# Agent attention and a leaky MLP on one core: the rest of the weight product, the linear part and the last weight tile move from the head into block 0

## The chip, the core and the metric

The program runs on one core of a Trainium2 chip. A core has five engines that run side by side and wait for each other by semaphores: TensorE (PE, matrix products; PEld is its loading of weights), VectorE (DVE), ScalarE (ACT), GpSimd (POOL) and SyncE (SP), which here only issues transfers. Each engine takes its instructions in the order in which they were written. The metric is the device time of one execution in microseconds (us). The kernel before took 963.24 us, the median of 3 runs (962.23 to 963.6).

## The reference

Cut to what is computed (2 batches of 12,480 tokens, 128 channels, 49 agents, 2,048 hidden units):

```python
def sm(a, b):                       # softmax of scaled scores
    s = scale * (a @ b.transpose(0, 2, 1))
    e = np.exp(s - s.max(-1, keepdims=True))
    return e / (e.sum(-1, keepdims=True) + 1e-09)
agent_v = sm(agents, k) @ v         # 49 x 128 per batch
x = sm(q, agents) @ agent_v         # 24,960 tokens x 128
h = x @ w_in                        # 128 -> 2,048
return np.maximum(0.01 * h, h) @ w_out
```

The weights arrive as 64-bit floats, everything else as 32-bit floats.

## The kernel before, in words

**What is multiplied.** For each batch the kernel forms M = agent_v @ w_in once, so that a token's hidden values are p @ M, where p are its 49 softmax weights towards the agents. The leaky step is split: 0.99 max(h, 0) goes through w_out (tiles wo_hi, wo_lo), and the linear rest 0.01 h @ w_out is one 128-column product with L = agent_v @ ww, ww = 0.01 w_in @ w_out. Every operand is kept as a high and a low part (m_hi and m_lo, l_hi and l_lo, hi and lo), so each product is three matmuls.

**Blocks.** The tokens go in 52 blocks of 480. A block has 8 steps; step p makes the hidden values of column pair p (256 of the 2,048): mm1 (6 matmul instructions on 64 rows, L748) into a two-bank PSUM tile h, of which there are two; relu on ACT (hi, L761) and on DVE (lo, L762); and, two steps later, mm2 (12 instructions, L778) into the block's output tile. Beside it, in fixed steps written with `at(step, function)`, run the softmax chains of the blocks to come (q_hi to p_dup, on ACT, POOL, PE and DVE) and the attention of the second batch. After each step's relu the `at` work of that step is written down, then mm2.

**The head** is all that comes before the first mm1. It loads k, v, q and the raw weights of batch 0, takes scores of agents against k (k_score; the running maximum k_run; k_copy), the maximum over all of them (k_max0 to k_max3), subtracts it (k_sub), exponentiates (k_exp) and sums up with v (k_av32, on PE), normalises (f_copy, f_den, f_tr, f_avT, f_rec), and makes M in four tiles of 512 columns: m_mm on PE, m_hi_of on ACT, m_lo_of on DVE. Beside that it converts the weights from 64-bit words in eight tiles w0 to w7 (even: w_in, odd: w_out): conv_bits (em and e, L246 and L247) on DVE, conv_mant and conv_exp on ACT (L314; L255 and L256), conv_low (L260), conv_sign (L267) and conv_mul (L274) on DVE, then wo_hi (ACT) and wo_lo (DVE). ww is summed up from transposed tiles of w_in (ww_tr L291, ww_copy L298, ww_mm L304).

**What sets the order.** In the head a planner (class Plan) does: each step has an engine, a cost in ns and the steps it follows; the step that can begin first is written next. Where PE would wait, it writes idle products on zeros (heat, L907). From block 0 on the order is written by hand. Tiles wait by buffers: raw weights, k and v of the head share one ring of 9 buffers (`ld`), so a load waits until the ninth load before it has been used up. The auxiliary PSUM tile (turn_82 or turn_83, the one that the block's output doesn't hold) serves every small product in turn.

Of the kernel before, what the change touches and what calls it, by code (L numbers as in the profile page):

```python
# [18 lines left out]
class Plan:  # L19


    def __init__(self, hop, start):
        self.hop, self.free, self.steps, self.done = hop, dict(start), {}, {}
        self.first = set()

    def add(self, name, eng, cost, fn, args, after):
        self.steps[name] = eng, cost, fn, args, after

    def emit(self, idle):
# [34 lines left out]
def tile_agent_attention_then_leaky_mlp(  # L64
# [31 lines left out]
    P = 128  # L96
# [84 lines left out]
    vr = [const.tile([TP, G, VW], F32R, name=f"vr{i}") for i in range(NVR)]  # L181
# [30 lines left out]
    def load_w(n):  # L212
        t = ld.tile([P, MC, 2], I32, tag="ld", name="w64")
# [82 lines left out]
    def ww_copy(n):  # L296
        t = rp.tile([P, MC], F32, tag="hi", name="wT")
# [160 lines left out]

    def av_zero(b, first):
# [56 lines left out]
    def m_parts(b, n):  # L516
# [5 lines left out]
        c = slice(n * MC, (n + 1) * MC)  # L522
        return m_hi[b][:, c], m_lo[b][:, c]

    def m_mm(b, n, pool=None, ps=None):
        if ps is not None:
            pass
        elif pool is None:
            ps = aux()
        else:  # L530
            if n % 2 == 0:
                mp_pair.append(pair("mp"))
            ps = mp_pair[-1][:, n % 2, :]
        ps, w = (ps, w_in_sb[:, n * MC:(n + 1) * MC]) if n < NM else (ps[:, :C], ww)
# [32 lines left out]
    def k_m(b, n):  # L567
        m_mm(b, n)
# [199 lines left out]
    def mm2(i, p):  # L768
# [15 lines left out]
        if p == NP // 2:  # L784
# [102 lines left out]
    with tc.manual_schedule():  # L887
# [8 lines left out]
        for t in vr:  # L896
            nc.gpsimd.memset(t[:, :, C:C + 1].bitcast(F32), 1.0)
            nc.gpsimd.memset(t[:, :, C + 1:C + 2].bitcast(F32), 0.0)
# [3 lines left out]
        avw.extend(halves(0))  # L902

        def heat(n, start=False):

            for i in range(n if ("wmm", NM - 1) not in plan.done else 0):
# [4 lines left out]
        plan = Plan(HOP, {"pe": 6000, "dve": 6500, "act": 2500, "pool": 5000, "dma": 3000})  # L911
# [4 lines left out]
        for o, a, n in SLOTS:  # L916
# [153 lines left out]
```

## Time and profile before

| | |
|---|---|
| median of 3 runs | 963.24 us (962.23 to 963.6) |
| the profiled execution | 963.1 us, its span 961.2 us |
| PE busy | 945.6 us, 98% of the span |
| DVE busy | 739.9 us, 77% |
| ACT busy | 612.3 us, 64% |
| POOL busy | 385.7 us, 40% |
| mean granted clock of PE | 0.998 of full speed |
| bytes moved by DMA | 70.00 MB, of them 20.87 MB before 70 us |

The span is what the profiler recorded of the program; the device time lies 1.9 us above it. The idle time of PE lies almost all in the first 78 us: PE is taken as busy where a matmul was under way, idle products included.

### The profile page before, as it was taken

How to read it: one execution, taken by the hardware profiler on the slowest of the kernel's cores; microseconds unless marked ns; L12 is line 12 of the kernel's file. 1: busy time of each engine (PE TensorE's matmuls, PEld its weight loads, DVE VectorE, ACT ScalarE, POOL GpSimd, SP SyncE). 2: the span in 40 equal slices, each digit the busy share in tenths (PEclk: the TensorE clock that was granted, in tenths of full speed). 3: DMA queues.
4: the chain of work that ended last, by engine and by line, in shares of the span. 5: the costliest groups of instructions: out<-in, count | busy, mean ns of one | idle time of the engine just before them, and what ended most of it. 6: DMA issues, size and time to landing. Idle time of an engine off the chain costs nothing.

```text
span 961.2 us, 22926 instructions
## 1 busy us (share of the span) xinstructions
PE 945.6 (98%) x9438; PEld 889.4 (93%) x9438; DVE 739.9 (77%) x1071; ACT 612.3 (64%) x907; POOL 385.7 (40%) x561
## 2 busy tenths in 40 slices
PE   8889999999999999999999999999999999999998
PEld 7768888889999999999888999999999999998997
DVE  7967767778888888888777777777777777777774
ACT  5756566656666666666676666666666666666654
POOL 3113233335556566564352434333343433343420
PEclk9999999999999999999999999999999999999999
DMA  9930422222312312321111111211111121112110
GB/s 349 380 140 12 130 79 83 66 60 64 94 53 63 94 53 73 85 63 53 32 42 52 43 53 32 62 32 53 42 43 52 43 53 42 52 42 54 32 42 22
DMA packets 28835, 70.00 MB, mean 73 GB/s; under 512 B 4387, under 2 KB 17955, under 8 KB 28731
## 3 DMA queue, kind: packets, MB, share of 16 engines
q1 hardware_dynamic: 28587, 68.42, 23.1%
q8 instruction: 74, 1.21, 0.6%
q14 instruction: 30, 0.25, 0.1%
q10 hardware_dynamic: 144, 0.12, 0.0%
HBM read 43.46 MB, written 12.78 MB: 59 GB/s over the span
## 4 chain that ended last, share of the span: by engine, by line
PE 95%; DVE 3%; DMA 1%; ACT 1%; SPq 0%; issue 0%; POOL 0%; ACTq 0%
PE turn L778 57%; PE h L748 28%; PE turn L622 2%; PE turn L789 2%; PE turn L355 1%; PE turn L447 1%; PE sc L355 1%; DMA kt<-in_k_dram 1%; DVE s_sb L321 1%; PE turn L471 1%; DVE lo L762 0%; PE mp L537 0%; PE turn L304 0%; DVE run L366 0%; PE turn L907 0%
## 5 line engine op out<-in xcount | busy, mean ns | idle before, releaser
L762 DVE SCALAR_TENSOR_TENSOR lo<-h,hi 128x960 fp32r<-128x960 f32 x416 | 478.8, 1151 | 188.4 <-ACT hi L761 188.4
L761 ACT ACTIVATE hi<-h 128x960 fp32r<-128x960 f32 x416 | 405.5, 975 | 292.6 <-PE h L748 266.6
L778 PE MATMUL turn<-hi,wo_hi 64*128 64x480 f32 x1664 | 410.5, 379 | 0.0
L778 PE MATMUL turn<-hi,wo_lo 64*128 64x480 f32 x1664 | 407.5, 376 | 0.0
L748 PE MATMUL h<-pT,m_hi 64*128 64x480 f32 x1664 | 325.7, 377 | 1.4 <-DVE lo L762 1.4
L778 PE MATMUL turn<-lo,wo_hi 64*128 64x480 f32 x1664 | 324.9, 375 | 0.0
L778 PEld LDWEIGHTS turn<-hi,wo_lo 64*128 64x128 f32 x1664 | 257.2, 184 | 7.6
L778 PEld LDWEIGHTS turn<-hi,wo_hi 64*128 64x128 f32 x1664 | 253.2, 184 | 8.0 <-issue 0.7
L778 PEld LDWEIGHTS turn<-lo,wo_hi 64*128 64x128 f32 x1664 | 228.9, 184 | 8.2
L748 PEld LDWEIGHTS h<-pT,m_hi 64*128 64x128 f32 x1664 | 227.0, 184 | 10.2 <-DVE lo L762 2.2
L748 PE MATMUL h<-pT,m_lo 64*128 64x480 f32 x832 | 232.0, 375 | 0.0
L748 PEld LDWEIGHTS h<-pT,m_lo 64*128 64x128 f32 x832 | 134.2, 184 | 4.6
L321 POOL TENSOR_TENSOR pT<-pt,pT 64x480 fp32r<-64x480 f32 (+1 forms) x52 | 63.7, 1226 | 77.1 <-ACT pT L724 77.1
L667 POOL COPY mx<-mx 32x15 f32<-32x15 f32 (+1 forms) x52 | 10.1, 195 | 188.5 <-DVE mx L662 184.2
L321 POOL TENSOR_TENSOR d<-st,mm 64x375 f32<-64x375 f32 (+1 forms) x52 | 43.8, 841 | 95.6 <-DVE mm L673 95.6
L321 POOL TENSOR_TENSOR qlo<-qt,qhi 128x480 fp32r<-128x480 f32 x52 | 64.0, 1231 | 32.8 <-ACT qhi L585 31.6
L812 POOL TENSOR_TENSOR oT<-oT 128x480 f32<-128x480 f32 x51 | 62.5, 1225 | 13.0 <-issue 10.0
L710 POOL TENSOR_TENSOR pd<-d,rs 64x375 f32<-64x375 f32 (+1 forms) x52 | 42.5, 818 | 31.9 <-DVE rs L705 31.9
L667 POOL COPY sm<-sm 32x15 f32<-32x15 f32 (+1 forms) x52 | 9.8, 189 | 106.3 <-DVE sm L690 106.3
L801 ACT COPY oT<-turn 128x480 f32<-128x480 f32 x102 | 51.9, 561 | 0.4 <-PE turn L778 0.4
L622 PE MATMUL turn<-qhi,a_hl 64*128 64x240 f32 x200 | 43.7, 271 | 1.0 <-ACT turn L607 1.0
L622 PE MATMUL turn<-qlo,a_hl 64*128 64x240 f32 x200 | 43.8, 271 | 0.0
(139 smaller groups left out, 905.2 us busy)
## 6 DMA issues: line engine op xcount, KB each, us to landing
qt<-in_q_dram SPq DMA_DIRECT2D x53, 240.0 KB, 2.9
kt<-in_k_dram SPq DMA_DIRECT2D x26, 480.0 KB, 7.5
out_dram<-oT SPq DMA_DIRECT2D x51, 240.0 KB, 2.0
pT<-pT SPq DMA_DIRECT2D x100, 120.0 KB, 2.3
vt<-in_v_dram SPq DMA_DIRECT2D x13, 520.0 KB, 8.4
vt<-in_v_dram SPq DMA_DIRECT2D x13, 487.5 KB, 4.7
w<-in_w_in_dram SPq DMA_DIRECT2D x4, 512.0 KB, 6.8
w<-in_w_out_dram SPq DMA_DIRECT2D x4, 512.0 KB, 8.0
```

The lines of the kernel that those rows point to most:

```text
L321: eng.tensor_tensor(out=o, in0=x, in1=y, op=ALU.subtract)
L355: nc.tensor.matmul(ps[r, j * NA:(j + 1) * NA], lhsT=k_t[b, c][:, j, r], rhs=a_sb[:, b, :], start=True, stop=True,)
L622: nc.tensor.matmul(s_t[i][:, m, :h], lhsT=a_hl[i // BPB][r], rhs=x[r, m * h:(m + 1) * h], start=(s == 0 and n == 0), stop=(n == 1), skip_g ...
L667: nc.gpsimd.tensor_copy(r[:n, :, 1], r[n:2 * n, :, 0])
L710: nc.gpsimd.tensor_tensor(out=pd[:n, :, :A0], in0=d[:n], in1=w[:n].to_broadcast([n, NT, A0]), op=ALU.mult,)
L748: nc.tensor.matmul(ps[:, g, :NB], lhsT=w[b][r, cols(2 * p + g)], rhs=t[r, x], start=(n == 0), stop=(n == 2),)
L761: nc.scalar.activation(hi, ps, AF.Relu)
L762: nc.vector.scalar_tensor_tensor(out=lo, in0=ps, scalar=0.0, in1=hi.bitcast(F32), op0=ALU.max, op1=ALU.subtract,)
L778: nc.tensor.matmul(o[g][:, :NB], lhsT=w[r], rhs=x[r], start=start, stop=stop)
L789: nc.tensor.matmul(o[g][:, :NB], lhsT=w[b][r], rhs=t[r, x], start=False, stop=False)
L801: nc.scalar.copy(t[:, g], o[g][:, :NB])
L812: nc.gpsimd.tensor_tensor(out=t[:, 0], in0=t[:, 0], in1=t[:, 1], op=ALU.add)
```

## The change

In the head, M stops after its first two tiles of 512 columns, and the first of these is made in two halves of 256 (m_half). The third tile is written right after the planned head (k_m(0, 2, 1)), the fourth in step 2 of block 0. The conversion of w7, the last tile of w_out, stands in steps 0 to 4 of block 0, and so do the last quarter of ww (ww_mm in step 3; ww_part and ww_end add the two sums) and L (step 5); the linear product of block 0 moves from its step 4 to its step 6. The softmax chain of block 1, which had been in block 0, is in the planned head as a whole. Raw weights get four tiles of their own (those that later hold vr), so the ring of 9 serves k and v alone; w7 takes the tile of w3. The load order and the planner's costs are new: a load is now an issue on SP, a trip and a transfer. In block 0 the two auxiliary tiles change places.

```diff
         done = self.done
         while len(done) < len(self.steps):
...
                     continue
                 ready = max((done[a] + self.hop for a in after), default=0)
-                key = max(ready, self.free[eng]), name not in self.first, -rest(name)
+                begin = max(ready, self.free.get(eng, 0))
+                key = begin + self.wait.get(name, 0), -rest(name), begin
                 if best is None or key < best[0]:
                     best = key, name
-            (begin, *_), name = best
-            eng, cost, fn, args, _ = self.steps[name]
-            if eng == idle[0] and begin > self.free[eng] + idle[2]:
+            (_, _, begin), name = best
+            eng, cost, fn, args, _, lag = self.steps[name]
+            if eng == idle[0] and begin > self.free.get(eng, 0) + idle[2]:
                 idle[1](round((begin - self.free[eng]) / idle[2]))
             fn(*args)
-            self.free[eng] = done[name] = begin + cost
+            self.free[eng] = begin + cost
+            done[name] = begin + cost + lag
 
...
 
-    ORDER = "qkwwkkkkkkkwkkkkkwvvvqwvvvvwqvwvvvvvw"
+    ORDER = "qkwwkkkkkkkwkkkkkvqvvvwvvwvwvvwvvvvwq"
     HOP = 90
...
     def aux():
...
     def halves(i):
 
         owner[0] = i
-        return [turns[i % 2][:, g, :] for g in range(2)]
+        return [turns[(i + 1) % 2][:, g, :] for g in range(2)]
 
     def pair(name):
...
     def load_w(n):
-        t = ld.tile([P, MC, 2], I32, tag="ld", name="w64")
+        t = const.tile([P, G * VW // 2, 2], I32, tag=f"vr{n % NVR}", name="w64")
+        t = t[:, :MC, :]
         m = n // 2
         if n % 2 == 0:
...
     def ww_copy(n):
-        t = rp.tile([P, MC], F32, tag="hi", name="wT")
+        if n < NM - 1:
+            t = rp.tile([P, MC], F32, tag="hi", name="wT")
+        else:
+            t = ld.tile([P, MC], F32, tag="ld", name="wT")
...
 
@@ -302,12 +309,19 @@
         for j in range(4):
             f = 4 * n + j
             nc.tensor.matmul(
-                avw[1][:, :C], lhsT=wT[n][:, j * P:(j + 1) * P], rhs=w_out_sb[:, f, :],
-                start=False, stop=(f == NF - 1),
+                avw[1][:, WW], lhsT=wT[n][:, j * P:(j + 1) * P], rhs=w_out_sb[:, f, :],
+                start=(n == NM - 1 and j == 0), stop=(f == NF - 1),
             )
 
+    def ww_part():
+        z = m_lo[1][:, :C]
+        nc.tensor.matmul(avw[1][:, WW], lhsT=z, rhs=z, start=False, stop=True)
+        nc.scalar.mul(ww, avw[1][:, WW], SLOPE)
+
     def ww_end():
-        nc.scalar.mul(ww, avw[1][:, :C], SLOPE)
+        nc.vector.scalar_tensor_tensor(
+            out=ww, in0=avw[1][:, WW], scalar=SLOPE, in1=ww, op0=ALU.mult, op1=ALU.add
+        )
...
 
+    def v_ones(r):
+        t = vr[r] = const.tile([TP, G, VW], F32R, tag=f"vr{r}", name="vr")
+        nc.gpsimd.memset(t[:, :, C:C + 1].bitcast(F32), 1.0)
+        nc.gpsimd.memset(t[:, :, C + 1:C + 2].bitcast(F32), 0.0)
...
             m_hi[b] = const.tile([P, DFF], F32R, tag="wm", name=f"m_hi{b}")
...
+        c = slice(int(n * MC), int(n * MC) + (MC if n == int(n) and b + n else MC // 2))
         return m_hi[b][:, c], m_lo[b][:, c]
 
-    def m_mm(b, n, pool=None, ps=None):
+    def m_half(b, h):
+
+        if h == 0:
+            mp_pair.append(pair("mp"))
+        c = slice(h * MC // 2, (h + 1) * MC // 2)
+        ps = mp_t[b, h / 2] = mp_pair[-1][:, 0, c]
...
+
...
         if ps is not None:
             pass
         elif pool is None:
-            ps = aux()
+            ps = aux2()[:, g, :]
         else:
-            if n % 2 == 0:
...
+        ps, w = (ps, w_in_sb[:, n * MC:(n + 1) * MC]) if n < NM else (ps[:, WW], ww)
         mp_t[b, n] = ps
...
             add(wo_lo[:, f, :], hi[:, g])
-        if p == NP // 2:
...
 
-    early = (0, 0, 0, 0, 0, 1, 1, 2, 2, 3, 4, 4, 5, 5, 6, 6, 6, 6)
+    w7 = 2 * NM - 1
+    at(0, conv_bits, w7)
+    at(0, conv_exp, w7)
+    at(1, conv_mant, w7, nc.scalar)
+    at(1, conv_low, w7)
+    at(1, conv_sign, w7)
+    at(2, k_m, 0, NM - 1, 0)
+    at(2, conv_mul, w7, nc.vector)
+    at(3, ww_mm, NM - 1)
+    at(3, ww_end)
+    at(3, wo_hi_of, w7, nc.scalar)
+    at(4, wo_lo_of, w7)
+    at(5, k_m, 0, NM, 1)
+    for x in range(NVR):
+        at(2 * NP + 2 * x, v_ones, x)
     for i in range(1, NBLK):
         at(NP * i + LAG, o_add, i - 1)
-    for r, (_, fn) in zip(early, chain[2:]):
-        at(r, fn, 1)
     for n in range(2, NBLK):
         for r, fn in chain:
             at(max(NP * n + r, 0), fn, n)
-    for i in range(2, NBLK):
+    for i in range(3, NBLK):
         at(max(NP * i - 20, 0), load_q, i)
-    for n in range(1, NM):
...
-            for i in range(n if ("wmm", NM - 1) not in plan.done else 0):
+            for i in range(n):
...
+            after = list(sent)
+            if what == "w":
+                after += [(y, c - NVR) for y in held["w"] if c >= NVR]
+            elif what != "q":
                 if len(ring) >= LD:
                     x, n = ring[-LD]
-                    after = [(y, n) for y in held[x]]
+                    after += [(y, n) for y in held[x]]
                 ring.append((what, c))
-            after += prev
-            prev = [(what, c)]
-            add((what, c), "dma", cost, fn, (c,), after)
+            sent = [("send", what, c)]
+            add(sent[0], "sp", 450, fn, (c,), after, lag=-HOP)
+            add(("trip", what, c), (what, c), 1500, lambda: None, (), sent)
+            if (what, c) == ("w", 0):
+                cost += 1700
+            add((what, c), "dma", cost, lambda: None, (), [("trip", what, c)] + come, lag=-HOP)
+            come = [(what, c)]
...
+        for n in range(w7):
             r = [("mul", n - RP)] if n >= RP else []
-            add(("bits", n), "dve", 940, conv_bits, (n,), [("w", n)] + r)
...
-            add(("mul", n), "dve", 600, conv_mul, (n, dve), [("low", n), ("sign", n)])
+            add(("sign", n), "dve", 620, conv_sign, (n,), [("exp", n)])
+            add(("mul", n), "dve", 620, conv_mul, (n, dve), [("low", n), ("sign", n)])
...
+                add(("wohi", n), "act", 530, wo_hi_of, (n, act), [("mul", n)])
+                add(("wolo", n), "dve", 600, wo_lo_of, (n,), [("wohi", n)])
...
+        for i in range(2):
+            last = ("q", i)
+            for n, (_, fn) in enumerate(chain):
+                eng, cost = costs[fn]
+                after = [last] + [(("chain", 0, 3 if n else 4))] * (i > 0 and n < 2)
+                add(("chain", i, n), eng, cost, fn, (i,), after)
+                last = ("chain", i, n)
...
+        for m in range(NM):
+            add(("tr", m), "pe", 1150, ww_tr, (m,), [("mul", 2 * m)])
+            add(("wcopy", m), "act", 500, ww_copy, (m,), [("tr", m)])
+            if m < NM - 1:
+                add(("wmm", m), "pe", 1000, ww_mm, (m,), [("wcopy", m), ("mul", 2 * m + 1), "avopen"] + [("wmm", m - 1)] * (m > 0))
...
-            add(fn, eng, cost, fn, (0,), [last] + [("s", NCH - 1, 1), ("wcopy", 1)] * (fn is k_max1))
+            add(fn, eng, cost, fn, (0,), [last] + [("s", NCH - 1, 1)] * (fn is k_max1))
...
-        costs = {
-            q_hi: ("act", 493), q_lo: ("pool", 1158), q_mm: ("pe", 403), q_x: ("act", 451),
...
-        last = ("q", 0)
-        for n, (_, fn) in enumerate(chain):
-            eng, cost = costs[fn]
-            add(("chain", n), eng, cost, fn, (0,), [last])
-            last = ("chain", n)
-        for n, fn in enumerate((q_hi, q_lo)):
-            eng, cost = costs[fn]
-            add(("chain1", n), eng, cost, fn, (1,), [("q", 1), ("chain", 4)] + [("chain1", 0)] * n)
...
-        for n in range(NM):
-            after = [f_avT, f_rec] + [("mm", n - 1)] * (n > 0)
-            add(("mm", n), "pe", 860, m_mm, (0, n, ps_h), after)
-            add(("mhi", n), "act", 520, m_hi_of, (0, n), [("mm", n)])
-            add(("mlo", n), "dve", 600, m_lo_of, (0, n), [("mhi", n)])
-            plan.first |= {("mhi", n), ("mlo", n), ("mm", n)}
-        plan.first |= {f_copy, f_rec, f_avT, f_den, f_tr, k_max0, k_max1d, k_max3}
-        plan.first |= {("run", c) for c in range(NCH)}
-        add("L", "pe", 250, k_m, (0, NM), ["ww", ("mlo", 0)])
+        last = f_avT
+        for n, fn, args in ((0, m_half, (0, 0)), (0.5, m_half, (0, 1)), (1, m_mm, (0, 1, ps_h))):
+            x = 1 if n < 1 else 2
+            add(("mm", n), "pe", 435 * x, fn, args, [last])
+            add(("mhi", n), "act", 120 + 240 * x, m_hi_of, (0, n), [("mm", n), f_rec])
+            add(("mlo", n), "dve", 140 + 265 * x, m_lo_of, (0, n), [("mhi", n)])
+            last = "mm", n
...
+        users = [
+            (("chain", 0, 2), ("chain", 0, 5)), (("tr", 0), ("wcopy", 0)),
...
+        ]
+        for (_, a), (b, _) in zip(users, users[1:]):
+            plan.steps[b][4].append(a)
...
         plan.emit(("pe", heat, 270))
+        ww_part()
+        k_m(0, 2, 1)
...
-                if i > 0 and f == LAG:
+                if f == LAG:
                     owner[0] = i
-                    o_copy(i - 1)
+                    if i > 0:
+                        o_copy(i - 1)
...
```

On PE at the end of the head, before (turn_82 holds ww and the idle products, turn_83 the small products, mp the tiles of M, h the hidden values):

```order
L498 MATMUL turn_83<-sel,avs 128x128
L907 MATMUL turn_82<-m_lo_102 128x512 x2
L537 MATMUL mp<-w_in_sb,avT 128x512 x2
L291 MATMUL turn_83<-ident,w_in_sb 128x128 x4
L537 MATMUL mp<-w_in_sb,avT 128x512
L291 MATMUL turn_83<-ident,w_in_sb 128x128 x4
L537 MATMUL mp<-w_in_sb,avT 128x512
L304 MATMUL turn_82<-w_out_sb,wT 128x128 x8
L537 MATMUL turn_83<-ww,avT 128x128
L748 MATMUL h<-pT,m_hi_100 128x480 x4
```

The same place now:

```order
L483 MATMUL turn_82<-m_lo_102 128x130
L311 MATMUL turn_82<-w_out_sb,wT 128x128 x4
L509 MATMUL turn_83<-avs,sel 128x1
L517 MATMUL turn_83<-sel,avs 128x128
L311 MATMUL turn_82<-w_out_sb,wT 128x128 x4
L550 MATMUL mp<-w_in_sb,avT 128x256 x2
L562 MATMUL mp<-w_in_sb,avT 128x512
L318 MATMUL turn_82<-m_lo_102 128x128
L562 MATMUL turn_83<-w_in_sb,avT 128x512
L773 MATMUL h<-pT,m_hi_100 128x480 x4
L773 MATMUL h<-pT,m_lo_101 128x480 x2
```

Two transposes and a ww product left the gaps between the M products, two ww products stand between the sum over v and M, and the first mm1 follows three products of M (two of them of half size) and the third tile's.

On ACT, from the last tiles of M in the head on, before:

```order
L558 ACTIVATE m_hi_100<-mp,rec 128x512
L310 ACTIVATE ww<-turn_82 128x128
L558 ACTIVATE l_hi_103<-turn_83,rec 128x128
L761 ACTIVATE hi<-h 128x960
L639 COPY sx<-turn_83 128x480
L585 CAST qhi<-qt 128x480
L761 ACTIVATE hi<-h 128x960 x3
L685 ACTIVATE d<-d 128x375
L607 COPY turn<-turn_83 128x2
```

Now:

```order
L583 ACTIVATE m_hi_100<-mp,rec 128x256 x2
L583 ACTIVATE m_hi_100<-mp,rec 128x512
L319 ACTIVATE ww<-turn_82 128x128
L583 ACTIVATE m_hi_100<-turn_83,rec 128x512
L786 ACTIVATE hi<-h 128x960
L259 ACTIVATE e<-e,off 128x512
L260 ACTIVATE e<-e,off 128x512
L610 CAST qhi<-qt 128x480
L786 ACTIVATE hi<-h 128x960
L328 ACTIVATE w_out_sb<-em 128x512
L786 ACTIVATE hi<-h 128x960
L583 ACTIVATE m_hi_100<-turn_82,rec 128x512
```

Between the first and the second hi of block 0 stand now both halves of conv_exp of w7 (e) and a qhi; before stood sx and qhi there.

On DVE, before, from the last m_lo on:

```order
L562 SCALAR_TENSOR_TENSOR m_lo_101<-mp,rec,m_hi_100 128x512 x2
L562 SCALAR_TENSOR_TENSOR l_lo_105<-turn_83,rec,l_hi_103 128x128
L762 SCALAR_TENSOR_TENSOR lo<-h,hi 128x960
L650 TENSOR_TENSOR sq<-turn_83,sx 128x480
L656 STREAM_TRANSPOSE st<-sq 128x480
L280 SCALAR_TENSOR_TENSOR wo_lo<-w_out_sb,wo_hi 128x512
L762 SCALAR_TENSOR_TENSOR lo<-h,hi 128x960
L662 TENSOR_REDUCE mx<-st 128x15
L280 SCALAR_TENSOR_TENSOR wo_lo<-w_out_sb,wo_hi 128x512
L762 SCALAR_TENSOR_TENSOR lo<-h,hi 128x960
```

Now:

```order
L587 SCALAR_TENSOR_TENSOR m_lo_101<-turn_83,rec,m_hi_100 128x512
L787 SCALAR_TENSOR_TENSOR lo<-h,hi 128x960
L250 TENSOR_SCALAR em<-w_821 128x512
L251 TENSOR_SCALAR e<-w_821 128x512
L787 SCALAR_TENSOR_TENSOR lo<-h,hi 128x960
L264 SCALAR_TENSOR_TENSOR w_out_sb<-w_821,w_out_sb 128x512
L271 SCALAR_TENSOR_TENSOR e<-w_821,e 128x512
L787 SCALAR_TENSOR_TENSOR lo<-h,hi 128x960
L587 SCALAR_TENSOR_TENSOR m_lo_101<-turn_82,rec,m_hi_100 128x512
L278 TENSOR_TENSOR w_out_sb<-w_out_sb,e 128x512
L787 SCALAR_TENSOR_TENSOR lo<-h,hi 128x960
L322 SCALAR_TENSOR_TENSOR ww<-turn_82,ww 128x128
```

The two bit steps of w7 (em, e) stand behind the first lo, its low and sign steps behind the second, its product and the m_lo of the fourth tile behind the third, and the sum of ww behind the fourth.

## Rows read from the trace of the kernel before

**Rows 1.** Windows: busy us per engine with instructions, granted clock, DMA share, GB/s.
```profile
24.00:34.00 10.00, 8.95 (x137) 7.26 (x137) 9.00 (x21) 6.42 (x13) 2.41 (x4) 1.00 1.03 405
34.00:44.00 10.00, 9.54 (x141) 8.39 (x139) 10.00 (x21) 8.69 (x18) 0.38 (x1) 1.00 0.97 340
44.00:54.40 10.40, 7.94 (x90) 7.01 (x89) 7.01 (x13) 5.18 (x11) 1.54 (x1) 0.84 0.95 371
54.40:63.40 9.00, 7.17 (x35) 4.38 (x34) 5.16 (x9) 6.30 (x11) 0.00 (x0) 1.00 0.38 131
63.40:78.00 14.60, 12.26 (x107) 9.38 (x106) 11.32 (x16) 8.11 (x12) 3.54 (x6) 1.00 0.00 1
78.00:961.00 883.00, 878.61 (x8593) 835.82 (x8591) 679.94 (x945) 565.49 (x824) 370.63 (x521) 1.00 0.20 56
```

**Rows 2.** Chain of waits, from M to the first mm1: start us, us, what.
```profile
54.50 1.88 PE mp L537 x4
...
56.40 0.70 ACT m_hi L558
...
57.12 0.76 DVE m_lo L562
...
60.84 1.80 PE turn L304 x16
...
63.48 0.88 PE h L748 x6
```

**Rows 3.** Chain of waits, block 0 up to the second batch's scores (L355).
```profile
64.38 0.98 ACT hi L761
...
65.38 1.16 DVE lo L762
66.54 0.57 DVE sq L650
...
73.60 0.50 PE turn L622 x4
74.10 1.30 PE turn L778 x12
75.39 0.65 PE h L748 x6
...
78.02 2.00 PE turn L355 x62
```

**Rows 4.** Chain of waits, from the maximum over the sums with v.
```profile
31.38 0.85 DVE e L267
...
32.70 0.59 DVE w_out_sb L260
...
33.42 1.51 DVE w_out_sb L274
34.93 2.86 DVE s_sb L321 x6
37.79 0.34 DVE em L246
38.13 0.36 DVE e L247
...
40.40 0.60 DVE e L267
...
44.49 0.72 ACT e L256
```

**Rows 5.** Groups of lines by form on DVE, 20 to 84 us: busy and mean, idle before.
```profile
L656 DVE STREAM_TRANSPOSE st<-sq 128x480 f32<-128x480 f32 x1 | 0.7, 678 | 0.0
...
L662 DVE TENSOR_REDUCE mx<-st 128x15 f32<-128x375 f32 x1 | 0.5, 528 | 0.0
```

**Rows 6.** Timeline: DVE products of two SBUF tiles beside POOL; start, duration, idle before.
```profile
46.77 0.69 DVE L274 TENSOR_TENSOR w_out_sb<-w_out_sb,e 128x512 f32<-128x512 f32 x1
...
48.18 1.54 POOL L321 TENSOR_TENSOR pT<-pt,pT 128x480 fp32r<-128x480 f32 x1 [13.80 <-ACT pT L724]
48.70 1.57 DVE L274 TENSOR_TENSOR w_in_sb<-w_in_sb,e 128x512 f32<-128x512 f32 x1
```

**Rows 7.** Timeline of PE: the last products with v.
```profile
47.24 5.22 PE L471 MATMUL turn<-vt,s_sb 120*49 120x130 f32 x64 [1.61 <-ACT e L256]
```

**Rows 8.** Window behind that wait, columns as in rows 1.
```profile
47.00:48.00 1.00, 0.76 (x8) 0.79 (x10) 1.00 (x3) 1.00 (x3) 0.00 (x0) 0.50 1.04 424
```

More of the change, by code (lines that the diff above doesn't have):

```diff
@@ L23, in __init__, with add @@
         self.hop, self.free, self.steps, self.done = hop, dict(start), {}, {}
-        self.first = set()
-    def add(self, name, eng, cost, fn, args, after):
-        self.steps[name] = eng, cost, fn, args, after
+        self.wait = {}
+    def add(self, name, eng, cost, fn, args, after, lag=80):
+        self.steps[name] = eng, cost, fn, args, after, lag
     def emit(self, idle):
@@ L47, in emit @@
             best = None
-            for name, (eng, cost, _, _, after) in self.steps.items():
+            for name, (eng, cost, _, _, after, _) in self.steps.items():
                 if name in done or any(a not in done for a in after):
@@ L180, in tile_agent_attention_then_leaky_mlp @@
     run = const.tile([TP, CH, NA], F32, name="run")
-    vr = [const.tile([TP, G, VW], F32R, name=f"vr{i}") for i in range(NVR)]
+    vr = [None] * NVR
     er = [const.tile([TP, G, EW], F32R, name=f"er{i}") for i in range(NER)]
@@ L783, in mm2 @@
             add(wo_lo[:, f, :], hi[:, g])
-        if p == NP // 2:
+        if p == (NP // 2 if i else NP - 2):
             t = pT_t[i]
@@ L895, in tile_agent_attention_then_leaky_mlp @@
         nc.vector.memset(off[:, 1:2], 255.0 * 2.0**23)
[L896 to L898 removed]
         for t in [pd] + er:
             nc.gpsimd.memset(t.bitcast(F32), 0.0)
[L902 removed]
+        avw.extend(turns[0][:, g, :] for g in range(2))
         def heat(n, start=False):
[L906 removed]
+            for i in range(n):
                 nc.tensor.matmul(
@@ L944, in tile_agent_attention_then_leaky_mlp @@
                 after += [("s", c, 0)] * g
-                add(("s", c, g), "pe", 480, k_score, (0, c, g, ps_h), after)
+                add(("s", c, g), "pe", 450, k_score, (0, c, g, ps_h), after, lag=150)
             after = [("s", c, 1)] + [("run", c - 1)] * (c > 0)
-            add(("run", c), "dve", 565, k_run, (0, c), after)
-            add(("copy", c), "act", 486, k_copy, (0, c), [("run", c)])
-        for n in range(2 * NM):
+            add(("run", c), "dve", 485, k_run, (0, c), after)
@@ new lines, in tile_agent_attention_then_leaky_mlp @@
+                add(("wolo", n), "dve", 600, wo_lo_of, (n,), [("wohi", n)])
+        costs = {
+            q_hi: ("act", 500), q_lo: ("pool", 1230), q_mm: ("pe", 700), q_x: ("act", 480),
+            q_add: ("dve", 580), q_tr: ("dve", 600), q_mm2: ("pe", 0), p_dup: ("pool", 0),
+            q_red: ("dve", 450), q_swap: ("pool", 430), q_mx: ("dve", 90),
+            q_sub: ("pool", 830), q_exp: ("act", 440), q_sum: ("dve", 440),
+            q_rec: ("dve", 580), q_norm: ("pool", 830), p_trans: ("dve", 590),
+            p_hi: ("act", 500), p_lo: ("pool", 1230),
+        }
@@ new lines, in tile_agent_attention_then_leaky_mlp @@
+        users = [
+            (("chain", 0, 2), ("chain", 0, 5)), (("tr", 0), ("wcopy", 0)),
+            (("tr", 1), ("wcopy", 1)), (k_max1, k_max1d), (k_max2, k_max3),
+            (("chain", 1, 2), ("chain", 1, 5)), (("tr", 2), ("wcopy", 2)),
+            (("tr", 3), ("wcopy", 3)), (f_den, f_avT),
+        ]
+        for (_, a), (b, _) in zip(users, users[1:]):
+            plan.steps[b][4].append(a)
+        slack = {
+            "tr": 100, "wmm": 300, "wohi": 400, "wolo": 300, "bits": 300, "mant": 300,
+            "exp": 400, "low": 600, "sign": 400, "mul": 200, "sub": 300, "e": 300, "copy": 400,
+        }
@@ L1016, in tile_agent_attention_then_leaky_mlp @@
+        for name in plan.steps:
+            if isinstance(name, tuple):
+                plan.wait[name] = slack.get(name[0], 300 * (name[:2] == ("chain", 1)))
         plan.emit(("pe", heat, 270))
+        ww_part()
+        k_m(0, 2, 1)
         steps = [(i, p) for i in range(NBLK) for p in range(NP)]
```

69 lines of the change are left out of this document (27 added, 42 removed).

## The prediction

> **What bounds the kernel now.** First the windows [rows 1]: from 78 us on PE is busy for 878.6 of 883.0 us at the full clock, so everything behind the scores of the second batch is a row of PE work without gaps, and the change leaves that work as it is. What happens ahead of the scores (start at 78.02 [rows 3]) moves the end one for one; nothing else does. So the whole forecast is one question: when do these scores start, 78.02 us now?
>
> Then the chain of waits backwards from there, in three stretches. M starts on PE at 54.50 and the first mm1 at 63.48 [rows 2]: nine microseconds in which the reader is to see PE products, ACT and DVE in turn (two tiles of M 1.88, m_hi .70, m_lo .76, and at the end two ww products, 1.80, between the last M product and mm1). Between 63.48 and 78.02 block 0 fills up [rows 3]: hi .98 and lo 1.16 are waited for before mm2 has anything to do. Ahead of M the chain lies on DVE, from the maximum over the scores at 33.42 on [rows 4]: subtractions (2.86 for six, .48 each) and the weight conversion. There the loads matter too: the DMA share is 1.03 at 24 to 34 us, .97 at 34 to 44 [rows 1], so weights arrive as fast as they can.
>
> **The change part by part.**
>
> *Up to the start of M.* Now DVE begins the subtractions about a microsecond earlier: before, a sign step of .85 and a low step of .59 stood between the maximum's steps [rows 4], and they are out of the way. Say 32.5. From there DVE has, by the new order, 13 subtractions (13 x .48 = 6.2), the conversion of four tiles w3 to w6, each em and e .70, low .60, sign .60 [rows 4] and mul .69 alone [rows 6], 2.59 in all (10.4 for four), and, new in this place, the softmax chain of block 1: sq .57 [rows 3], two transposes at .6, two reductions at .5 [rows 5], the four small ones taken as one more reduction: 3.3. Together 19.9, so DVE is through at 52.4 if it never waits. The weights allow that: the transfers of raw weights no longer wait for k's buffers, and the stretch 34 to 44 moved 340 GB/s where the one before it moved 405 [rows 1]; at 405 the same bytes take 1.6 us less, so the last weight tile of the head is there some 2 us earlier. I cost the loads at nothing for this reason; w7's transfer waits until w3 has been used, but is wanted only in block 0, by then at 62.7 (8.1 behind M's start, see below).
>
> DVE does not run alone, though. The chain brings POOL steps of its own (d, pd, pT) into this stretch. Where POOL's pT ran beside a mul, the mul took 1.57 instead of .69 [rows 6], .88 more. Three such meetings are 2.6, none is 0; I take one and a third, 1.2: only pT, the last step of the chain, has muls right behind it in the new order, and the third stands for the chance that d or pd meets one. That gives 53.6. Behind the last mul stand a ww product (.90 [rows 2]) and two wo_hi on ACT before the normalised sum reaches PE: M starts at 54.6, so **+0.1** against 54.50. Bounds: 52.4 (no meeting, the ww product in time) to 56.1 (three meetings).
>
> A page bears on the POOL term. The Trainium skill, "SBUF — State Buffer", section "Who interferes with whom", has a DVE instruction with two SBUF inputs contend with any GpSimd instruction that reads SBUF, the one that starts first holding the shared ports for its whole length. The mul of 1.57 agrees with it. By it every one of the three POOL steps that meets such a DVE step delays it, M starts at 56.0, and the total is 969.0 instead of 967.6.
>
> *From M to the first mm1.* Before, 63.48 - 54.50 = 9.0. Now a first half product (.47, half of .94 [rows 2]), its m_hi (.48, between half and all of .70), its m_lo (.48, between half and all of .76), and on PE behind the halves and the tile of 512 the first mm1. PE has .47 + .47 + .1, then the third product waits until the PSUM pair is free again (the first m_lo), .94, and small steps between: mm1 at 4.0. Since the waits for ww, the fourth tile and L are gone from here, this stretch is **5.0 shorter**. It is not yet a gain, because ACT is not done: m_hi of both halves (.48 each), m_hi of the second tile .70, ww .28 (128 columns, under the .35 of half a tile), m_hi of the third tile .70, with the waits between: the first hi can begin only 6.0 after M's start, two after mm1.
>
> *Block 0.* The new order on ACT and DVE decides. From 6.0: hi .98, lo 1.16, then em and e .70 behind the first lo, on which ACT's exp (two halves of .72 [rows 4]) waits; the exp and a qhi (480 columns, .6 by m_hi's .70 for 512) stand ahead of the second hi. So hi .98 and lo 1.16 again come after .70 + 1.44 + .6: 6.0 + 7.0 = 13.0. The fourth mm1 needs the tile of hidden values that this lo frees, and PE waits from 11.0 to 13.0; before, sx and a qhi stood between the two hi. Then DVE has low .60, sign .60, lo 1.16, m_lo .76 and mul .69 in its row, 3.8, to 16.8: that mul makes w7, and the last ww product, in step 3 on PE, waits for it. PE has work to 13.7 and idles for 3.1; queued behind that ww product are q_mm of block 2, mm2 and every mm1 to come. Then the ww product .90 and a hop .2, ww_end .3 (behind a lo): 18.2. q_mm (.50 [rows 3]) writes to the tile that ww_end reads: 18.75. mm2 1.30 and mm1 .65 and hops .3: 21.0. hi, lo: 23.1. wo_lo .57 and sq .57: 24.3. L waits for the PSUM tile that sq reads, .4: 24.7. mm2 1.30, mm1 .65: the scores start 26.7 after M, where it was 78.02 - 54.50 = 23.5. That is **+3.2**, with the 5.0 already in it. Its bounds: -5.0, if ACT and DVE hide w7 altogether and block 0 fills as before from its first mm1, and +5.4, if each of the nine steps of w7, ww and L in the row costs a quarter of a microsecond more, as one sign step of .85 did against one of .60 [rows 4].
>
> *The clock.* After 1.61 us of idle PE [rows 7] the granted clock fell to .50 [rows 8], the lower of two levels (1.2 against 2.4 GHz); the mean over 44 to 54.4 is .84 [rows 1], so some 3.3 us ran at half speed ((1 - .84) x 10.4 / .5), which loses 1.7. The new waits, 2.0 and 3.1 us long, are of that length. Part of the loss would fall into stretches in which PE waits anyway: I take **+1.2**, between 0 and 3.4 (both waits, 1.7 each).
>
> Sum: the profiled execution took 963.1 us, .14 under the median of the runs. 963.1 + 0.1 + 3.2 + 1.2 = 967.6.
>
> **The rivals.**
>
> *Faster: M's split pays in full.* If the w7 steps lie in DVE's free time of block 0 (DVE was busy for 11.32 of 14.6 us there [rows 1], and chain 1's steps have left it), block 0 runs from its first mm1 as before: 963.1 + 0.1 - 5.0 = 958.2. For it: the DVE work added to block 0 (4.2 for w7, m_lo and ww) is hardly more than what was taken out (3.3 and two wo_lo). Against it: it is not the sum that counts but the row, with exp before the second hi and the ww product on PE. It decides if the gap before the fourth mm1 is under half a microsecond. .14.
>
> *No change: the head gains what block 0 loses.* If POOL and DVE don't meet and the clock holds, M starts at 52.4: 963.1 - 2.1 + 3.2 = 964.2. For it: loads are 2 us earlier, and a mul alone takes .69 [rows 6]. Against it: the chain of block 1 lies in the same stretch. .18.
>
> *Worse by the clock.* Both waits of block 0 drop it: 963.1 + 0.1 + 3.2 + 3.4 = 969.8. For it: .50 after a shorter wait [rows 7, 8]. Against it: 1.00 at 54 to 63, in spite of 1.8 us of PE idle there [rows 1]. .08.
>
> *Worse by POOL.* Three meetings of .88 ahead of M: 963.1 + 1.5 + 3.2 + 1.2 = 969.0. For it: the 1.57 [rows 6]. Against it: the mul beside pT is the only step in the rows read here that was hit, and d and pd work on fewer elements (375 of 480 a row). .07.
>
> **How the numbers follow.** Forecast .53, its own range 965.3 to 969.5; faster .14, no change .18, worse .15. A difference under 0.2% (1.9 us) can't be told from no change, so faster means below 961.3, slower above 965.2. The faster case lies wholly in the first, the no-change case in the second, and the rest in the third: .14, .18, .68. The range 960.5 to 971.5 leaves out most of the faster case (.12) and the ends of the clock's (3.4 plus a late M: .05).
>
> **What would show it.** M's start near 54.6 with DVE busy without gaps from the maximum on; the first mm1 4.0 behind M, the first hi 6.0; in block 0 PE idle for about 2 us ahead of its fourth mm1, released by lo, and about 3 us ahead of the last ww product, released by mul; a granted clock of .5 behind one of them; the scores' start at 82.5. It is wrong if the second hi is not behind exp, if the ww product doesn't wait for mul, or if M starts before 53: then the time is below 965.

## The result, and the profile after

The changed kernel took 973.96 us (median of 4 runs; 971.59 to 975.34) against 963.08 (median of 4): a ratio of 1.0111, interval 1.009 to 1.0133. It is 10.9 us slower, where +4.5 was forecast and 971.5 was the end of the range. Its profiled execution took 974.26 us, its span is 972.4.

The windows of the changed kernel, columns as in [rows 1], cut at M's start, the first mm1 and the scores of the second batch:

```profile
24.00:34.00 10.00, 8.34 (x135) 6.30 (x135) 8.02 (x15) 5.24 (x11) 2.29 (x2) 1.00 1.02 407
34.00:44.00 10.00, 9.05 (x149) 8.07 (x145) 10.00 (x23) 9.55 (x20) 1.64 (x3) 1.00 1.03 408
44.00:54.40 10.40, 5.71 (x79) 4.46 (x74) 9.90 (x18) 6.01 (x11) 3.42 (x4) 1.00 0.31 122
54.40:59.10 4.70, 4.31 (x21) 4.02 (x22) 2.78 (x6) 1.58 (x4) 0.00 (x0) 0.59 0.86 255
59.10:65.74 6.64, 5.56 (x12) 2.27 (x10) 0.97 (x2) 1.66 (x4) 0.00 (x0) 0.52 0.69 271
65.74:89.53 23.79, 16.81 (x112) 12.15 (x114) 13.60 (x19) 11.09 (x17) 1.22 (x1) 0.86 0.00 1
89.53:972.00 882.47, 878.41 (x8591) 838.78 (x8591) 678.34 (x939) 565.46 (x823) 369.12 (x527) 1.00 0.20 56
```

The last row answers to the last of [rows 1]: from the scores on nothing changed (878.41 of 882.47 us busy, 878.61 of 883.00 before). The scores start at 89.53, not 78.02, and these 11.5 us are the loss (11.2 in the two profiled executions). The loads are faster, as worked out (408 GB/s from 34 to 44 us, 340 before), and DVE is busy for 9.90 of 10.40 us ahead of M. What is new is the clock: .59, .52 and .86 behind 54.4 us, where [rows 1] has 1.00. (The kernel before has its fall earlier: .84 from 44 to 54.4, where the changed one has 1.00.) Cut finer, the changed kernel shows two falls to .50, one ahead of M that lasts into the first mm1, and one that begins in PE's wait for w7; between them, at 66 to 75 us, the clock is at 1.00:

```profile
55.00:56.00 1.00, 0.81 (x6) 0.52 (x4) 0.69 (x1) 0.15 (x1) 0.00 (x0) 0.60 0.96 217
...
65.00:66.00 1.00, 1.00 (x6) 0.30 (x6) 0.25 (x1) 0.97 (x3) 0.00 (x0) 0.78 0.01 4
...
74.00:75.00 1.00, 0.50 (x6) 0.09 (x2) 1.00 (x3) 0.75 (x2) 0.00 (x0) 1.00 0.00 0
...
76.00:77.00 1.00, 0.00 (x0) 0.00 (x0) 1.00 (x3) 0.00 (x0) 0.00 (x0) 0.50 0.00 0
```

The chain of waits of the changed kernel, to hold against [rows 2, 3] (start us, us, what):

```profile
54.43 1.40 PE turn L311 x8
...
57.40 1.71 PE turn L311 x8
59.10 1.72 PE mp L550 x4
...
61.89 2.08 PE mp L562 x2
...
65.74 0.88 PE h L773 x6
...
77.10 2.09 PE turn L311 x8
...
80.43 2.32 PE turn L803 x12
...
89.53 2.00 PE turn L369 x62
```

One ww product (L311, x8) took .90 before and takes 1.40, 1.71 and 2.09; two halves of M 1.72 where two whole tiles took 1.88; an mm2 2.32 for 1.30. Two ww products now stand ahead of M.

DVE and POOL of the changed kernel ahead of M, picked from the timeline (start, duration, then idle before):

```profile
42.52 0.95 POOL L335 TENSOR_TENSOR d<-st,mm 128x375 f32<-128x375 f32 x1 [0.46 <-DVE mm L698]
48.56 1.05 POOL L735 TENSOR_TENSOR pd<-d,rs 128x375 f32<-128x375 f32 x1 [0.89 <-DVE rs L730]
51.45 1.66 POOL L335 TENSOR_TENSOR pT<-pt,pT 128x480 fp32r<-128x480 f32 x1 [1.84 <-ACT pT L749]
```
```profile
41.92 0.43 DVE L251 TENSOR_SCALAR e<-w 128x512 int32<-128x512 int32 x1
42.68 1.06 DVE L251 TENSOR_SCALAR e<-w 128x512 int32<-128x512 int32 x1
48.85 1.30 DVE L264 SCALAR_TENSOR_TENSOR w_in_sb<-w,w_in_sb 128x512 f32<-128x512 uint32 x1
51.96 1.69 DVE L264 SCALAR_TENSOR_TENSOR w_out_sb<-w,w_out_sb 128x512 f32<-128x512 uint32 x1
53.68 0.69 DVE L278 TENSOR_TENSOR w_out_sb<-w_out_sb,e 128x512 f32<-128x512 f32 x1
54.29 0.68 DVE L264 SCALAR_TENSOR_TENSOR w_out_sb<-w,w_out_sb 128x512 f32<-128x512 uint32 x1
55.01 0.69 DVE L278 TENSOR_TENSOR w_out_sb<-w_out_sb,e 128x512 f32<-128x512 f32 x1
```

Each of chain 1's three POOL steps met a DVE step: 1.06 for .43, 1.30 and 1.69 for .68, in all 2.3 us. The last two lines with L278 are the last two products of the weight conversion ahead of M: they end at 54.37 and 55.70.

PE's waits in block 0 of the changed kernel (timeline; the wait in us and its releaser in brackets):

```profile
73.58 0.70 PE L773 MATMUL h<-pT,m_hi 64*128 64x480 f32 x4 [1.24 <-DVE lo L787]
...
77.10 2.07 PE L311 MATMUL turn<-w_out_sb,wT 128*128 128x128 f32 x8 [2.60 <-DVE w_out_sb L278]
```

Both waits that the prediction named are there, with the releasers it named.

### The profile page after: what moved, and what is told of

Same layout as the page of the kernel before. It is cut to its first block, busy times and chain, and to the rows that moved or that the text cites. A ratio compares the mean times of both kernels' runs of the same rounds, so it can differ in the third digit from the quotient of the medians.

```text
span 972.4 us, 22908 instructions
## 1 busy us (share of the span) xinstructions
PE 949.2 (98%) x9428; PEld 893.4 (92%) x9428; DVE 741.7 (76%) x1073; ACT 612.3 (63%) x908; POOL 386.0 (40%) x561
## 4 chain that ended last, share of the span: by engine, by line
PE 94%; DVE 4%; ACT 1%; DMA 1%; issue 1%; POOL 0%; ACTq 0%; DVEq 0%; POOLq 0%
PE turn L803 57%; PE h L773 27%; PE turn L647 2%; PE turn L814 2%; PE turn L369 1%; PE turn L461 1%; DMA w<-in_w_in_dram 1%; PE turn L939 1%; DVE run L380 1%; PE turn L311 1%; PE sc L369 0%; DVE lo L787 0%; DVE e L271 0%; ACT hi L786 0%; DVE w_out_sb L264 0%
## 5 line engine op out<-in xcount | busy, mean ns | idle before, releaser
L773 PE MATMUL h<-pT,m_lo 64*128 64x480 f32 x832 | 229.4, 375 | 0.0
```

The source lines that it names most:

```text
L773: nc.tensor.matmul(ps[:, g, :NB], lhsT=w[b][r, cols(2 * p + g)], rhs=t[r, x], start=(n == 0), stop=(n == 2),)
```

## The experiments

All start from the changed kernel. For each: M's start, the first mm1 and the scores in its profile, that execution's time, and the median of its runs, 4 to 12 of them (the kernel before stood at 962.8 to 963.2 beside them).

| kernel | M | mm1 | scores | profiled | median |
|---|---|---|---|---|---|
| before | 54.4 | 63.4 | 78.0 | 963.1 | 963.1 |
| changed | 58.9 | 65.7 | 89.5 | 974.3 | 973.96 |
| idle products, many | 57.2 | 61.4 | 84.7 | 970.4 | 969.14 |
| idle products, spread | 57.2 | 61.3 | 83.3 | 968.5 | 968.41 |
| idle products ahead of M alone | 57.7 | 61.9 | 85.3 | 970.5 | 970.65 |
| chain 1 in block 0 | 53.6 | 57.7 | 82.4 | 967.3 | 968.03 |
| w7 in the head | 58.3 | 62.4 | 84.9 | 969.7 | 967.86 |
| w7 later in block 0 | 58.9 | 65.7 | 91.9 | 976.7 | 974.08 |
| chain 1's POOL steps on DVE | 55.9 | 60.0 | 83.4 | 968.2 | 970.25 |
| M's first tile whole | 58.8 | 63.6 | 87.2 | 972.0 | 971.04 |
| chain 1 and w7 back | 55.2 | 59.4 | 79.7 | 965.2 | 964.28 |
| ... and four steps moved | 55.1 | 59.3 | 79.3 | 964.2 | 964.05 |
| ... and M's tile whole | 55.1 | 58.0 | 77.4 | 962.4 | 962.20 |
| ... and PE's order | 54.8 | 61.3 | 78.1 | 963.1 | 960.88 |

**The clock.** Idle products on zeros at PE's waits, of the kind

```diff
+        if n >= 2:
+            heat(6)          # ww_tr; also ahead of ww_mm(1)
...
+                if s == 3:
+                    heat0(5)     # ahead of the fourth mm1
+    at(3, heat0, 11)             # ahead of the last ww product
     at(3, ww_mm, NM - 1)
```

> The changed kernel, with idle products on zeros written where PE waits: six ahead of the transposes of the third and fourth weight tile and six ahead of the second ww product, all before M; five ahead of block 0's fourth mm1 and eleven ahead of the last ww product. Theory (the clock): PE's waits of 1.5 us ahead of M and of 2.6 us in block 0 let the granted clock fall to .50, and the work that then stands on the path runs at half speed; in the changed kernel's trace the ww products take 1.40, 1.71 and 2.09 us, M to the first mm1 6.6 us, one mm2 2.32. With the clock held M starts at 57.8 (59.1 before), the first mm1 4.2 behind it, and block 0 is 2.4 shorter: some 6 us less, about 968. Rival (the order of ACT and DVE alone sets the time, PE's speed lies beside it): less than 1 us, 973 to 975.

969.14: 4.8 us of the 10.9. The clock still fell once in block 0 (.50 from 65 to 68 us), and the eleven ran on for 1.5 us after w7's product was there. With 2, 4, 3 and 9 products ahead of the second, third, fourth mm1 and the ww product:

> The changed kernel with idle products in more places and fewer of them each than in the first run of this kind (969.14, in which the clock still fell to .50 for 4 us in block 0, and some 1.5 us of idle products stood on the path): the same three sixes ahead of M, two and four ahead of block 0's second and third mm1, three ahead of the fourth, nine ahead of the last ww product. Theory (the clock): it stays up, and the time is 966 to 967.5. Rival (the rest is waits alone): no further gain, 968.5 to 970.

968.41, and the windows of this kernel (M to mm1, mm1 to the scores) show the clock at 1.00 in both:

```profile
57.30:61.37 4.07, 2.99 (x12) 1.30 (x10) 1.70 (x4) 0.95 (x2) 0.00 (x0) 1.00 0.92 321
61.37:83.38 22.01, 19.36 (x130) 13.51 (x132) 13.64 (x20) 11.67 (x18) 1.22 (x1) 1.00 0.12 47
```

So the clock is worth 5.55 us here, less what the idle products themselves cost. The spread won .7 us over the first run of this kind, where the theory had asked for 1.6 to 3.1: with the clock held, the rest of the loss, 5.5 us, is not the clock. By place:

> The changed kernel with the three sixes of idle products ahead of M alone, none in block 0 (with those too: 968.41 and 969.14). Theory (two falls of the clock, each with its price): the first fall goes, M starts at 57.3 (59.1) and mm1 4 us behind it (6.6), the second stays: 969.5 to 971. Rival (all of the gain comes from one place): 968.5, or 973 and more.

970.65: about 3.3 us belong to the fall ahead of M, 2.2 to the one in block 0.

**Chain 1 back in block 0.**

```diff
-            for n, (_, fn) in enumerate(chain):
+            for n, (_, fn) in enumerate(chain[:2] if i else chain):
...
+    early = (0, 0, 0, 0, 0, 1, 1, 2, 2, 3, 4, 4, 5, 5, 6, 6, 6, 6)
+    for r, (_, fn) in zip(early, chain[2:]):
+        at(r, fn, 1)
```

> The changed kernel, with the softmax chain of block 1 behind its first two steps put back into block 0, in the steps where it was. Theory (DVE and POOL ahead of M): 3.3 us of DVE work and the three meetings with POOL (e 1.06 beside d, low 1.30 beside pd, low 1.69 beside pT: 2.2 us over their usual length) leave the stretch before M, which starts some 4 us earlier, at 55; block 0 gets sx, sq, st and the rest of the chain and is 1 to 2 us longer: 970 to 972. Rival (the weights' arrival or the ACT chain sets M's start): M at 58 or later, and the time 974 or more, since block 0 is longer.

968.03, better than the theory: M starts 5.3 us earlier, and the clock doesn't fall there (1.00 from 44 us to mm1), where PE waits .72 us ahead of the last transposes instead of 1.55, and not at all ahead of the first ww product. In block 0 the wait for w7 is there as before, 3.05 us where it was 2.60:

```profile
70.58 1.16 PE L311 MATMUL turn<-w_out_sb,wT 128*128 128x128 f32 x8 [3.05 <-DVE w_out_sb L278]
```

**POOL's meetings.**

```diff
-        sub(nc.gpsimd, d[:n], t[:n, :, :A0], ...)
+        eng = nc.vector if i == 1 else nc.gpsimd     # so too pd, pT and their place in the plan
+        sub(eng, d[:n], t[:n, :, :A0], ...)
```

> The changed kernel, with block 1's three large POOL steps (d, pd, pT) on DVE instead, in the head as before: no POOL instruction meets a DVE one there. DVE gets 1.5 us more work of its own and loses 2.25 us of meetings (e 1.06 for .42, low 1.30 and 1.69 for .68). Theory (the meetings are real stalls of DVE): DVE is through with the last product .5 to 1 us earlier, 53.5 to 53.9 against 54.38, and every DVE step of one form there takes the same time; the time is 972.5 to 973.5. Rival (the long instructions are an artefact of the profile): DVE is through 1.5 us later, 975 to 976.

The last product but one ends at 53.50 instead of 54.37 and the last at 54.83 instead of 55.70, .9 earlier, as the theory said (its 54.38 is the last but one), though DVE has 1.8 us more to do; and the low steps are back at .69:

```profile
50.76 0.69 DVE L264 SCALAR_TENSOR_TENSOR w_in_sb<-w,w_in_sb 128x512 f32<-128x512 uint32 x1
...
52.09 0.69 DVE L264 SCALAR_TENSOR_TENSOR w_out_sb<-w,w_out_sb 128x512 f32<-128x512 uint32 x1
52.81 0.69 DVE L278 TENSOR_TENSOR w_out_sb<-w_out_sb,e 128x512 f32<-128x512 f32 x1
...
54.14 0.69 DVE L278 TENSOR_TENSOR w_out_sb<-w_out_sb,e 128x512 f32<-128x512 f32 x1
```

The time fell by more than the theory's 972.5 to 973.5, to 970.25: in the profiled execution (968.2, the shortest of its runs) the clock didn't fall ahead of M. The meetings are real stalls; their own price is the .9 and the 1.8 together, 2.6 us.

**w7 back in the head**, so that its conversion falls beside M's products:

```diff
-    at(0, conv_bits, w7)
-    at(0, conv_exp, w7)      # and the four steps after it
...
-        for n in range(w7):
+        for n in range(w7 + 1):
```

> The changed kernel, with the conversion of w7 (em to the product) in the planned head, where it falls beside M's products; its wo_hi, wo_lo, the last ww product and L stay in block 0. Theory (w7's row of steps makes the waits of block 0): the waits of 1.24 and 2.60 us on PE go, the second fall of the clock with them; M to the first mm1 gets up to 1 us longer: 5 to 6 us less, about 968.5. Rival (block 0 waits for something else, or what is taken away there comes back as later m_hi and m_lo): within 1.5 us of the changed kernel, 972.5 or more.

967.86, near the theory's 968.5, but this median lies between two pairs of executions: 965.97 and 966.31 with a mean granted clock of 1.0 and .999, 969.41 and 969.74 with .994. The profiled one is of the second pair. In it M to mm1 took 4.1 us at the full clock, so w7 found room there, and the waits for w7 are gone. But the second fall of the clock is not: PE waits 1.49 us for an m_lo ahead of its second mm1 and 1.40 for a lo ahead of its third, and the clock is at .50 from 66 to 72 us. So the waits for w7 went, as the theory said; the falls of the clock went, by the mean clocks, in the two short executions alone.

**w7 later in block 0.**

```diff
-    at(0, conv_exp, w7)
+    at(1, conv_exp, w7)      # low and sign 1 -> 2, the product 2 -> 3
-    at(3, ww_mm, NM - 1)
+    at(4, ww_mm, NM - 1)     # behind q_add of block 2
```

> The changed kernel, with the w7 steps in block 0 but further back: exp behind the second hi instead of ahead of it, low and sign a step later, the product a step later, the last ww product and the sum of ww in step 4 behind block 2's q_add. Theory (the places in the rows of ACT, DVE and PE cost, not the work): the second lo is there 2 us earlier, PE doesn't wait 2.6 us for w7, the clock stays up in block 0: 4 to 6 us less, 968 to 970. Rival (the work itself is too much for DVE in block 0, wherever it stands): within 1.5 us of the changed kernel.

A miss: 974.08, again a median between two pairs, 970.95 and 971.49, and 976.68 twice. The profile is of one of the long ones. In it the second lo came 2.4 us earlier, but two new waits took the place of the old one, both for a reader of the auxiliary tile:

```profile
76.04 0.57 PE L647 MATMUL turn<-qhi,a_hl 64*128 64x240 f32 x2 [2.98 <-DVE m_lo L587]
...
83.36 2.08 PE L311 MATMUL turn<-w_out_sb,wT 128*128 128x128 f32 x8 [3.19 <-DVE sq L673]
```

M's fourth tile, ww, q_mm, L and the scores take turns in the auxiliary PSUM tile, and here two of them wait until DVE has read the one before. Moving w7's steps back moved the wait into this queue. Whether the short executions had these waits too, no trace shows.

**Both edits.**

> The two edits that helped alone, together: the chain of block 1 back in block 0 (alone 968.03) and the conversion of w7 back in the planned head (alone 967.86), against 973.96 of the changed kernel. What is left of the change is the split of M, its last two tiles, the last ww product and L in block 0, and the tiles and the order of the loads. Theory (two separate costs, one ahead of M and one in block 0): M starts near 53.5, first mm1 4 to 4.5 behind it, block 0 without the waits for w7: the gains add up, 961 to 963.5. Rival (both took away the same fall of the clock): they do not add, 966 to 968.

964.28, between the theory's range and the rival's: alone they won 5.9 and 6.1, together 9.7. Most adds up, 2.3 us do not. That both had brought back the same part of the clock is likely but not shown.

**M's split.** Four steps of that kernel were moved first, and then the halves undone:

```diff
+            late = [f_avT] * (n == w7)                # w7's ACT steps
-    at(2, k_m, 0, NM - 1, 0)
+    at(0, m_mm, 0, NM - 1, None, turns[0][:, 0, :])   # m_hi, m_lo in step 2
...
-        for n, fn, args in ((0, m_half, (0, 0)), (0.5, m_half, (0, 1)), (1, m_mm, ...
+        for n, fn, args in ((0, m_mm, (0, 0, ps_h)), (1, m_mm, ...
```

> The kernel with both edits undone (964.28), and four steps moved: w7's two ACT steps wait for the copy of the normalised sum, so that they no longer stand ahead of it; no idle products once the sum over v is complete (two pairs of .72 us stood on the path there); M's fourth product goes to step 0, into PE's wait of 1.50 us; wo_lo of w7 goes behind L, so that the q_add which L waits for is .6 earlier, with three idle products ahead of L, where the clock fell (2.64 instead of 2.00 us for the scores, 1.84 and 1.20 instead of 1.50 and .66 before). Theory (these are waits on the path): M starts at 53.6 (55.18), block 0 is 1.0 + .6 + 1.9 shorter: 959 to 960.5, under the kernel before. Rival (each of the waits hides another one, late m_hi, lo or PSUM readers): 962 to 964.

> The same kernel as the one before it in this call, with M's first tile whole (512 columns) as in the kernel before the change, not in two halves. Theory (the halves shorten the way to the first mm1): PE waits 1.08 us for the first half's m_lo before it can write the second tile, so the halves win little: 0 to 0.8 us. Rival (the halves are worth the 1 us or more that M's first m_hi and m_lo take less): over 1 us slower without them.

964.05 with halves, 962.20 without (ratios to before 1.0012, 1.0003 to 1.0021, and .9995, .9986 to 1.0003). The four moves won next to nothing by themselves (964.28 before them; their theory had asked for 959 to 960.5), as their rival said; and both views on the split were wrong: whole tiles are 1.85 us faster. PE with halves, then with whole tiles:

```profile
55.08 1.13 PE L550 MATMUL mp<-w_in_sb,avT 128*128 128x256 f32 x4 [0.62 <-ACT avT L529]
57.30 1.13 PE L562 MATMUL mp<-w_in_sb,avT 128*128 128x512 f32 x2 [1.08 <-DVE m_lo L587]
...
59.32 0.70 PE L773 MATMUL h<-pT,m_hi 64*128 64x480 f32 x4
```
```profile
55.10 1.98 PE L564 MATMUL mp<-w_in_sb,avT 128*128 128x512 f32 x4 [0.62 <-ACT avT L529]
...
57.99 0.70 PE L775 MATMUL h<-pT,m_hi 64*128 64x480 f32 x4
```

The halves share the PSUM pair with the second tile: its product waits 1.08 us for the first half's m_lo, and the second half's m_hi waits for that product, on ACT:

```profile
58.46 0.47 ACT L583 ACTIVATE m_hi<-mp,rec 128x256 fp32r<-128x256 f32 x1 [1.74 <-PE mp L562]
```

Whole tiles go back to back. The changed kernel with this alone:

> The changed kernel with M's first tile whole instead of in two halves, and nothing else. Theory (the halves cost: the second tile's product waits for the first half's m_lo, the second half's m_hi for that product): M to the first mm1 is 1.3 us shorter at the full clock, more at the lower one, 971 to 972.5. Rival (in the changed kernel the third tile and the lower clock hide it): 973.5 to 974.5.

971.04, 2.9 us faster than with halves, as the theory said (the runs, 969.18 to 972.92, overlap with those of the changed kernel, 971.59 to 975.34; in the profiles M to mm1 takes 4.7 us instead of 6.8).

**PE's order, on top of that.**

```diff
-... + [("wmm", m - 1)] * (m > 0))
+... + [("wmm", m - 1)] * (m > 0) + [("mm", 1)] * (m == 2))
...
                 mm2(*steps[s - LAG])
+            if s == 3:
+                ww_mm(NM - 1)
+                ww_end()
+                q_mm(2)
```

> The kernel with whole M tiles and both edits undone (962.2), with two places more: the third ww product behind M's second product (it stood for 1.16 us on PE ahead of the transposing of the sum), and, in block 0, the last ww product, the sum of ww and block 2's q_mm behind step 3's mm2 instead of ahead of it (PE waited there 1.25 us for the fourth m_lo and .47 for the sum); no idle products in block 0. Theory (PE's row of instructions is what makes these waits, and mm2 can fill them): M starts at 53.9 (55.10), the scores of the second batch at 74.5 to 75.5 (77.49): 959 to 960.5, faster than the kernel before. Rival (the waits move to the next user of the auxiliary tile, L or q_add): 961.5 to 962.5.

960.88, faster than the kernel before (.998, .9971 to .9989). The theory's 959 to 960.5 was missed by .4, and M's start moved less than expected. Its profiled execution (963.1) was the slowest of its runs; the clock fell in it ahead of M (two M tiles in 3.78 us), so it shows the new order but not the median. The other runs have no trace, but their mean granted clocks fit: .996 in the profiled one and those of 962.40 and 962.51, .998 or .999 in the other eight (959.64 to 962.84).

## Why the prediction was wrong

The direction, the place and the bound were right, the size was not: 967.6 against 973.96. By its own terms, with the kernel whose clock stayed up as the measure for all but the clock:

- **M's start: +0.1 forecast, +2.8 at the full clock (57.32 against 54.50).** The step that failed is "Behind the last mul stand a ww product (.90) and two wo_hi". The new order that I had read shows two ww products there, and between them the copy of the sum, its denominator and its transpose. M follows the last product but one, on which the first of the two ww products waits, and this takes 3.2 us, not 1.0. In the chain of waits of the kernel whose clock stayed up:

```profile
53.45 0.70 DVE w_out_sb L278
...
54.20 1.17 PE turn L317 x8
...
55.40 0.28 ACT avs L505
...
56.43 0.89 PE turn L317 x8
57.32 0.88 PE mp L556 x4
```

  DVE's row was too short as well: its last product ends at 55.70 in the changed kernel, not at 53.6. The first subtraction began at 33.12 instead of 32.5, and the POOL meetings took 2.3 us, not 1.2: the count of one and a third was wrong, all three met a DVE step. The Trainium skill ("SBUF — State Buffer", "Who interferes with whom") has a DVE instruction with two SBUF inputs contend with a GpSimd one that reads SBUF. Two of the three meetings agree with it (1.30 and 1.69 for .68); the third met a step with a single SBUF input (1.06 for .43).
- **From M to mm1: 4.0 forecast, 4.07 at the full clock.** Right as a number, 6.64 in the changed kernel. In part this is luck: the sum names 2.4 us of it, and the product of the third tile, which stands ahead of mm1 on PE and takes 1.07, is in it only as "small steps". That the split pays was wrong: the forecast had the wait for the first m_lo in its sum, and did not ask what whole tiles would take (2.9 us, 55.10 to 57.99). All that was won came from taking ww, the fourth tile and L out of the way.
- **Block 0: from M to the scores 26.7 forecast, 26.1 at the full clock.** The row through exp, the second lo, w7's product, the last ww product, ww_end, q_mm and L is the measured one, step by step, in the chain of waits of that kernel. Single waits of the changed kernel were shorter (1.24 and 2.60 for 2.0 and 3.1).
- **The clock: +1.2 forecast, +5.55 measured.** This is the largest error, 4.35 of 6.4 us. The term that failed is the one for PE's idle time: I looked for it in block 0 alone. But DVE full ahead of M means PE waiting for it, 5.71 of 10.40 us busy where it had been 7.94, with waits of 1.46, 1.55 and 1.55 us. The clock fell there too, and its mean is .59 and .52 in the stretches in which PE's products are the chain. This fall alone took 3.3 us; the one in block 0 took 2.2.

The sum: 967.6 + 2.7 - .6 + 4.35 = 974.05, the measured 973.96 within the runs' scatter. The clock's term is the difference of two medians, so the sum tests only the other two: without the clock they give 968.5, and 968.41 was measured. Of the rivals, "worse by POOL" was true in its condition (three meetings, 2.3 us for its 2.6). "Worse by the clock" was not: of the two waits that it names in block 0 only the second dropped the clock, and the larger fall lay ahead of M, where no rival looked. "M's split pays in full" is refuted by the 1.24 us ahead of the fourth mm1, where it wanted under half a microsecond, and by the whole tiles; "no change", which needed M at 52.4, by M's start in every run that kept chain 1 in the head (55.9 or later).

Not tried: the new load order and tiles alone on the kernel before. That they are worth something rests only on 408 against 340 GB/s and M's start at 53.6 with chain 1 out of the way.

## What to carry to other kernels

When work moves onto an engine that is already full ahead of a chain of small products, price the waits it makes on TensorE a second time: the products behind them may run at half speed, and that was half of this loss (5.55 of 10.9 us). A product cut in halves gained nothing here, where both halves and the next product share a PSUM tile whose readers and writers take turns. Count every instruction of the new order between the last bound step and the one that is waited for, not only the kinds that the change names.

## What the hardware showed unexpectedly

- PE's waits ahead of M in the changed kernel were 1.46, 1.55 and 1.55 us, and the clock fell from about 55.2 on (.60 from 55 to 56 us, .50 in the next nine); in the kernel before, 1.8 us of idle time in 9.0 (54.4 to 63.4) left it at 1.00. Filling the waits with idle products kept it at 1.00 for both stretches.
- A POOL subtraction of two SBUF tiles also stretched a DVE step with a single input (e, 1.06 for .43), not only those with two.
